# Row sums applied to the exponentials before they are turned; 5 of 16 copies between quadrants issued by ScalarE

## Chip, cores and metric

One core of one Trainium2 chip. The time is that of one launch in device microseconds (us); the kernel before is given as the median of three runs, and its profile is of one further execution. Smaller is better.

## What is computed

All arrays are float32. B, H, S, D = 4, 8, 576, 64; 2304 tokens, d_model 512, d_ff 2048.

```python
scores = scale * q @ k.T                               # per batch and head, 576 x 576
thresh = max(scores, axis=-1) - tau
scores = where(scores >= thresh, scores, -1e9)
attn   = exp(scores - max(scores, axis=-1))
attn   = attn / (sum(attn, axis=-1) + 1e-9)
x      = attn @ v                                      # then heads side by side: 2304 x 512
h = x @ w_in;   x = where(h > 0, h, exp(min(h, 0)) - 1) @ w_out      # first layer
h = x @ w2_in;  out = max(0.01 * h, h) @ w2_out                      # second layer
```

## The kernel before, in words

**Stages.** The first stage, up to about 520 us of the span, is the attention, with part of the first layer laid between its steps (7 blocks of 256 tokens, the first half of d_ff). Then come the rest of the first layer and the second layer, which are almost nothing but matmuls in blocks of 512 tokens.

**Attention.** The work is cut into 32 *groups*: 8 token ranges (4 or 5 *units* of 64 query rows each) times 4 pairs of heads; 144 units in all. `group` (line 417) issues the loads of k, q and v on SyncE's queue (SP), then its units. A unit (line 435) runs, for 64 query rows of both heads on 128 partitions: the scores `s` by TensorE (PE; line 442); scale and row extreme into `ss` by VectorE (DVE; 446); threshold `thr` by DVE or GpSimd (POOL; 449, 451); mask and exponential `e` by ScalarE (ACT; 454, 457), the latter with the row sum `su`; then `e` has to be turned so that keys lie on partitions. In the first 4 groups PE turns it (472). In the other 28, DVE turns 32 x 32 blocks within each quadrant of 32 partitions (464, `e` to `t`), and 16 DMA copies move the blocks between quadrants (486, `t` to `p`). These copies can begin when all units of the group are turned. Then PE multiplies `p` with `v` (496) and DVE multiplies the result with the reciprocal row sums `rb` into `x` (504). Buffers: 2 each of `t`, `p`, `e`, `k`, `q`, `v`, `s`; 3 of `ss`; one PSUM bank for the product with `v`.

**Row sums.** After the product the query rows lie along the free axis, so the reciprocals have to be turned and spread too. `row_sums` (line 509) does it once a group: reciprocal (511) and a 32 x 32 transpose (512) on DVE, a store to DRAM (513), and two loads that broadcast it over 64 partitions each (515), all on SP's queue. Line 504 waits for these loads.

**Order.** The source does not fix the order of instructions. A list scheduler (`Order.run`) places every step by readiness, by a due time (offsets in the table `KN`) and by an assumed cost, and picks an engine where a step has alternatives (`ka`, `kx`, `kg`, ... in `KN` name them: P, A, D for POOL, ACT, DVE). On the chip each engine works through its own list strictly in that order. The assumed cost of a DMA issue on SP is `ISSUE`.

**The two MLP layers.** Steps `h` (548; PSUM `h` and `hb`) and `y` (591) are float32 products made of three passes over a high and a low part (`xh`, `xl`, `gh`, `gl`, `wih`, ...), which ACT, DVE and POOL split (helpers in lines 298 to 310). The second half of the first layer's weights is loaded and split once the attention has ended.

Of the kernel before, what the change touches and what calls it, by code (L numbers as in the profile page):

```python
# [10 lines left out]
F32 = mybir.dt.float32  # L11
# [10 lines left out]
NP = NH // 2  # L22
# [11 lines left out]
BESIDE = 7  # L34
GP = 1
SX = 640
LAG = 2
# [5 lines left out]
KN = dict(  # L43
    pad=18, stay=3577.21, late=1.3, margin=0, look=0.00390102, warm=3, tu=2231.35, lead=16053.3, wv0=828.315,
    wv1=194.793, early=4257.91, boff=24778.1, bdt=4649.72, yoff=2581.02, coff=-6478.49, wb=1663.97, w2a=5835.19,
    o1=-2909.85, o2=1357, o3=2931.81, o4=-3826.63, o5=5331.7, o6=-25.7749, mo=-10678.1, ka='PA', kl='PAD', kh='PA',
    ko='D', kt='DP', kx='A', kxl='DP', km='DP', kg='AD', kgl='P', kgl1='D', kd='P', kc='AD')

# [41 lines left out]
class Order:  # L90
# [5 lines left out]
    def op(self, alts, deps=(), uses=(), vt=0.0, lat=0.0):  # L96
        o = Op()
        o.alts = alts if isinstance(alts, list) else [alts]
        o.deps, o.vt, o.lat = [d for d in deps if d is not None], vt, lat
        o.outs, o.done, o.eng, o.seq = [], None, None, len(self.ops)  # L100
        for g in uses:
            if g.back is not None:
                o.deps.append(g.back)
            if not g.users and g.before is not None:
                o.deps.append(g.before.users[0])
            g.users.append(o)
        self.ops.append(o)
        return o

    def run(self):  # L110
        for o in self.ops:
            deps = set()
            for d in o.deps:
                deps.update(d.users if isinstance(d, Gen) else (d,))
# [111 lines left out]
LAND = 2100.0  # L226
ISSUE = 350
HALFP = 105
# [20 lines left out]
def moved(packets, size):  # L249
    return packets * (6 + size * 0.0385) / 16 * 1.35  # L250

@with_exitstack
def attn_moe_kernel(ctx, tc, qT, kT, vn, tau, w1i, w1o, w2i, w2o, yp, rsd, out):
    nc = tc.nc
# [34 lines left out]

    def sp(packets, size, fn):  # L290
        return (SP, ISSUE, fn, moved(packets, size))

# [69 lines left out]
    k_r = ring(ap_, 2, [128, 2, HALF], F32, "k")  # L362
    q_r = ring(ap_, 2, [128, 2, 64 * UM], F32, "q")
    v_r = ring(ap_, 2, [128, 2, 5, D], F32, "v")
# [7 lines left out]
    e_r = Ring(itertools.cycle(es_).__next__, 2)  # L372
    ident = ac.tile([128, 128], F32, name="ident")
    make_identity(nc, ident)
    sm_r = {t: ring(ap_, 4, [128, 1], F32, t) for t in ("nm", "thr")}
    su_r = ring(ap_, 3, [128, UM], F32, "su")
    rc_r = Ring(None, 2)
    st_r = ring(ap_, 2, [128, 32], F32, "st")
    rb_r = ring(ap_, 2, [128, 64 * UM], F32, "rb")

# [5 lines left out]
    ss_r.make = itertools.cycle(sts).__next__  # L386
    sus = [ac.tile([128, 32], F32, name=f"rc{j}") for j in range(2)]
    for t in sus:
        nc.vector.memset(t, 1.0)
    rc_r.make = itertools.cycle(sus).__next__  # L390
    wz = sts[0]
# [22 lines left out]
    xready = {}  # L414
    slot = itertools.count()

    def group(gi, p, vts):
# [9 lines left out]
        by_pe = gi < GP  # L427
        su, pg, tg = su_r.new(), p_r.new(), None if by_pe else t_r.new()
        done, turned = [], []

# [3 lines left out]
        def unit(j, vt):  # L434
            s, ss, e = s_r.new(), ss_r.new(), e_r.new()
            nm, thr = (sm_r[t].new() for t in ("nm", "thr"))

            def qk():
                for h in range(2):
                    for i in range(2):  # L440
                        r = slice(64 * i, 64 * i + 64)
                        nc.tensor.matmul(s()[64 * h:64 * h + 64, i, 0:HALF], q()[r, h, 64 * j:64 * j + 64],  # L442
                                         k()[r, h], start=True, stop=True)
# [13 lines left out]
            o = op((ACT, act(S) + 190, lambda: nc.scalar.activation(  # L457
                out=e()[:, 0:S + 1], in_=ss()[:, 0:S + 1], func=AF.Exp, bias=taun, accum_out=su()[:, j:j + 1])),
                [o], [ss, e, su], vt + KN["o2"])
            done.append(o)  # L460
            cols = slice(32 * j, 32 * j + 32)

            if not by_pe:
# [3 lines left out]
                return  # L467
            t = ya.new()

# [12 lines left out]
        vt = vts[n - 1] + KN["o3"]  # L482
        rb, rgot = row_sums(gi * NE + p, n, su, done, vt + 500)
        got = turned
        if not by_pe:
            got = [op(sp(32, 20 * w, lambda a=a, d=d: nc.sync.dma_start(  # L486
                out=pg()[32 * d:32 * d + 32, 5 * a * w:5 * a * w + 5 * w],
                in_=tg()[32 * a:32 * a + 32, 5 * d * w:5 * d * w + 5 * w])), turned, [pg, tg], vt + KN["o4"])
                for a in range(4) for d in range(4)]
            vt += KN["o5"]  # L490
# [10 lines left out]
        def split(a):  # L501
            return a.rearrange("p (h u i) -> p h u i", h=2, i=32)

        xready[gi, p] = op((DVE, dve(64 * n), lambda: nc.vector.tensor_tensor(
            out=x[:, p, b * S + 64 * u0:b * S + 64 * u1].rearrange("p (u h i) -> p h u i", h=2, i=32),
            in0=split(ps()[:, 0:64 * n]), in1=split(rb()[:, 0:64 * n]), op=ALU.mult)),
            [o, *rgot], [ps, rb], vt + KN["o6"] + 500)

    def row_sums(at, n, su, done, vt):
        rb, st, rc = rb_r.new(), st_r.new(), rc_r.new()  # L510
        o = op((DVE, 140, lambda: nc.vector.reciprocal(out=rc()[:, 0:n], in_=su()[:, 0:n])), done, [su, rc], vt)
        o = op((DVE, 140, lambda: nc.vector.transpose(out=st(), in_=rc())), [o], [rc, st], vt)
        o = op(sp(128, 128, lambda: nc.sync.dma_start(out=rsd[at].rearrange("a u i -> (a u) i"), in_=st())),
               [o], [st], vt)
        got = [op(sp(128, 128 * n, lambda h=h: nc.sync.dma_start(  # L515
            out=rb()[64 * h:64 * h + 64, 0:64 * n].rearrange("p (a q) -> p a q", a=2),
            in_=rsd[at, 2 * h:2 * h + 2, 0:n].rearrange("a u i -> a (u i)").partition_broadcast(64))),
            [o], [rb], vt) for h in range(2)]
        return rb, got

# [256 lines left out]
```

## Time and profile before

| | |
|---|---|
| median of 3 runs | 1160.18 us (1159.62 to 1168.07) |
| the profiled execution | 1164.52 us, its span in the trace 1162.7 us |
| busy: PE / DVE / ACT / POOL | 1051.9 / 586.6 / 508.0 / 157.5 us |
| busy share of the 16 DMA engines, SP's and ACT's common queue kind | 37.9% of the span |

A busy share over the whole span mixes the attention stage with the MLP stages, so the stages are read apart. "SPq" is the queue of SyncE, on which an entry is one DMA issue; the time a transfer takes afterwards is not in it. Issuing DMAs isn't counted as busy time of any engine. The releaser of a wait is inferred; of several that could have ended it, the latest is named.

### The profile page before, as it was taken

The page shows a single profiled execution, that of the slowest core. Times are in us where ns is not written, and L with a number is a line of the kernel's source. Part 1 is how long each engine was busy: PE and PEld are TensorE (multiplying, and loading weights), DVE is VectorE, ACT ScalarE, POOL GpSimd, SP SyncE. Part 2 cuts the span into 40 slices and gives each one's busy share as a digit, 9 for nine tenths or more (in the row PEclk, how much of TensorE's full clock was granted, in tenths as well). Part 3 has the DMA queues.
Part 4 walks back from the last instruction along what each step waited for, and adds up shares of the span by engine and source line. Part 5 has one row for each costly group of instructions (what it writes and reads, how often), then busy time and mean ns, then how long its engine had stood idle before and what let it go on. Part 6 is the DMA issues. An engine that isn't in the chain of part 4 may idle for free.

```text
span 1162.7 us, 17064 instructions
## 1 busy us (share of the span) xinstructions
PE 1051.9 (90%) x6294; PEld 814.4 (70%) x6294; DVE 586.6 (50%) x1201; ACT 508.0 (44%) x1006; POOL 157.5 (14%) x278
## 2 busy tenths in 40 slices
PE   7778777787788778889999999999999999999998
PEld 3455455555566555558888888988888888888898
DVE  6876555655566556628888943686121121121121
ACT  6976555555455555515655532453221221221221
POOL 3454121222111122100111100010000000000000
PEclk9989898989899889989999999999999999999999
DMA  6676666656666666543544411132000000000000
GB/s 217 195 214 178 171 179 178 176 136 179 158 176 158 162 178 176 152 123 109 161 132 161 146 36 37 56 120 79 1 37 1 1 37 1 1 37 1 1 37 20
DMA packets 72435, 125.39 MB, mean 108 GB/s; under 512 B 16032, under 2 KB 37024, under 8 KB 72352
## 3 DMA queue, kind: packets, MB, share of 16 engines
q1 hardware_dynamic: 72352, 124.30, 37.9%
q8 instruction: 50, 0.82, 0.3%
q14 instruction: 33, 0.27, 0.1%
HBM read 72.35 MB, written 9.96 MB: 71 GB/s over the span
## 4 chain that ended last, share of the span: by engine, by line
PE 65%; SPq 15%; DMA 9%; DVE 5%; issue 3%; ACT 2%; POOL 0%; DVEq 0%; ACTq 0%; POOLq 0%
PE y L591 29%; PE h L548 15%; PE hb L548 13%; SPq L486 13%; PE v L496 6%; DMA rb<-rsd_dram 2%; DMA rsd_dram<-st 2%; DMA wraw<-in_w1i_dram 2%; PE s L442 2%; DVE ss L446 2%; DMA p<-t 2%; DVE t L464 1%; ACT e L457 1%; SPq L515 1%; SPq L426 1%
## 5 line engine op out<-in xcount | busy, mean ns | idle before, releaser
L591 PE MATMUL y<-gh,woh 128*128 128x512 f32 (+1 forms) x736 | 255.6, 347 | 2.1 <-ACT ysx L309 1.4
L591 PE MATMUL y<-gl,woh 128*128 128x512 f32 (+1 forms) x736 | 251.4, 342 | 0.0
L591 PE MATMUL y<-gh,wol 128*128 128x512 f32 (+1 forms) x736 | 251.3, 341 | 0.0
L298 DVE TENSOR_TENSOR gl<-g,gh 128x512 fp32r<-128x512 f32 (+1 forms) x128 | 83.3, 651 | 270.6 <-ACT g L574 260.9
L496 PE MATMUL v<-p,v 128*64 128x320 f32 (+1 forms) x640 | 127.9, 496 | 68.8 <-DMA rsd_dram<-st 39.1
L548 PE MATMUL h<-xh,wih 128*128 128x256 f32 (+1 forms) x480 | 164.6, 343 | 14.1 <-DVE g L567 9.4
L591 PEld LDWEIGHTS y<-gh,woh 128*128 128x128 f32 x736 | 138.5, 188 | 34.7 <-issue 14.4
L548 PE MATMUL h<-xl,wih 128*128 128x256 f32 (+1 forms) x480 | 159.0, 331 | 1.3 <-POOL xl L299 1.0
L548 PE MATMUL h<-xh,wil 128*128 128x256 f32 (+1 forms) x480 | 158.3, 330 | 0.0
L454 ACT ACTIVATE ss<-ss,thr 128x576 f32<-128x576 f32 x144 | 110.3, 768 | 105.5 <-DVE thr L451 58.2
L591 PEld LDWEIGHTS y<-gl,woh 128*128 128x128 f32 x736 | 138.6, 188 | 16.2
L591 PEld LDWEIGHTS y<-gh,wol 128*128 128x128 f32 x736 | 138.6, 188 | 16.2
L496 PEld LDWEIGHTS v<-p,v 128*64 128x64 f32 x640 | 62.7, 162 | 122.5 <-issue 64.1
L446 DVE TENSOR_SCALAR_CACHE_REDUCE ss<-s,scl 128x576 f32<-128x576 f32 x144 | 115.1, 800 | 46.6 <-PE s L442 45.3
L464 DVE STREAM_TRANSPOSE t<-e 128x640 f32<-128x640 f32 x128 | 106.7, 839 | 44.7 <-DMA rsd_dram<-st 19.0
L548 PEld LDWEIGHTS h<-xh,wih 128*128 128x128 f32 x480 | 91.6, 191 | 43.4 <-DVE g L567 12.3
L457 ACT ACTIVATE e<-ss,taun 128x577 f32<-128x577 f32 x144 | 111.5, 774 | 13.4 <-DVE t L464 11.1
L442 PE MATMUL s<-k,q 64*64 64x288 f32 x1152 | 97.6, 442 | 12.9 <-DVE ss L446 8.7
L548 PEld LDWEIGHTS h<-xl,wih 128*128 128x128 f32 x480 | 91.8, 191 | 10.2 <-POOL xl L299 1.5
L548 PEld LDWEIGHTS h<-xh,wil 128*128 128x128 f32 x480 | 91.9, 191 | 8.2
L548 PE MATMUL hb<-xl,wih 128*128 128x512 f32 (+1 forms) x256 | 94.5, 369 | 0.0
L548 PE MATMUL hb<-xh,wil 128*128 128x512 f32 (+1 forms) x256 | 94.5, 369 | 0.0
(438 smaller groups left out, 1139.7 us busy)
## 6 DMA issues: line engine op xcount, KB each, us to landing
p<-t SPq DMA_DIRECT2D x256, 100.0 KB, 2.2
p<-t SPq DMA_DIRECT2D x192, 80.0 KB, 2.4
v<-in_vn_dram SPq DMA_DIRECT2D x32, 320.0 KB, 3.7
k<-in_kT_dram SPq DMA_DIRECT2D x32, 288.0 KB, 3.0
wraw<-in_w1i_dram SPq DMA_DIRECT2D x16, 512.0 KB, 4.4
wraw<-in_w1o_dram SPq DMA_DIRECT2D x16, 512.0 KB, 3.6
wraw<-in_w2i_dram SPq DMA_DIRECT2D x16, 512.0 KB, 3.5
wraw<-in_w2o_dram SPq DMA_DIRECT2D x16, 512.0 KB, 3.4
```

The source lines that it names most:

```text
L298: return pick(who, D=(dve(n), lambda: nc.vector.tensor_tensor(**args()), PORT), P=(pool_tt(n), lambda: nc.gpsimd.tensor_tensor(**args())))
L426: lv = op(sp(128, 2560, lambda: nc.sync.dma_start(out=v(), in_=vn[hp])), [], [v], due + 8e3)
L442: nc.tensor.matmul(s()[64 * h:64 * h + 64, i, 0:HALF], q()[r, h, 64 * j:64 * j + 64], k()[r, h], start=True, stop=True)
L446: o = op((DVE, dve(S) + 160, lambda: nc.vector.tensor_scalar(out=ss()[:, 0:S].rearrange("p (j c) -> p j c", j=2), in0=s()[:, :, 0:HALF], s ...
L454: o = op((ACT, act(S) + 95, lambda: nc.scalar.activation(out=ss()[:, 0:S], in_=ss()[:, 0:S], func=AF.Prelu, bias=thr(), scale=-1.0, alpha= ...
L457: o = op((ACT, act(S) + 190, lambda: nc.scalar.activation(out=e()[:, 0:S + 1], in_=ss()[:, 0:S + 1], func=AF.Exp, bias=taun, accum_out=su( ...
L464: turned.append(op((DVE, dve(SX) + 70, lambda: nc.vector.transpose(out=blocks(tg).rearrange("p d c q -> p c d q")[:, :, :, cols], in_=e(). ...
L486: got = [op(sp(32, 20 * w, lambda a=a, d=d: nc.sync.dma_start(out=pg()[32 * d:32 * d + 32, 5 * a * w:5 * a * w + 5 * w], in_=tg()[32 * a:3 ...
L496: nc.tensor.matmul(ps()[64 * h:64 * h + 64, 0:64 * n], v()[:, h, c, :], blocks(pg)[:, 2 * h:2 * h + 2, c], start=(c == 0), stop=(c == 4))
L515: got = [op(sp(128, 128 * n, lambda h=h: nc.sync.dma_start(out=rb()[64 * h:64 * h + 64, 0:64 * n].rearrange("p (a q) -> p a q", a=2), in_= ...
L548: nc.tensor.matmul(hp(), w_()[:, cs], x_()[:, 0:tb], start=(k == 0 and z == 0), stop=(k == KC - 1 and z == 2))
L591: nc.tensor.matmul(ysl(yg, m), w_()[:, cs], g_()[:, 0:tb], start=(first and z == 0 and share == 0), stop=(last and z == 2 and end))
```

## The change

The reciprocal of each unit's row sum is taken on DVE right after the exponential, and `e` is multiplied with it before it is turned; `row_sums`, its store and its two loads a group go, and the product with `v` is copied to `x` by ACT (`kv='A'`). `kn='P'` gives the new multiplication to POOL. Of a group's 16 copies 5 are issued by ACT (`NA`), spread over the 16. `e` gets a third buffer. q is laid out so that a group's load has 128 pieces in place of 256. The scheduler's table has new due times and other choices of engine, and assumes 640 for a copy's issue on SP (before 350) and 300 on ACT.

```diff
+NA = 5
+ACTI = 300
...
-    o1=-2909.85, o2=1357, o3=2931.81, o4=-3826.63, o5=5331.7, o6=-25.7749, mo=-10678.1, ka='PA', kl='PAD', kh='PA',
-    ko='D', kt='DP', kx='A', kxl='DP', km='DP', kg='AD', kgl='P', kgl1='D', kd='P', kc='AD')
+    o1=-2774.74, o2=2563.78, o3=4792.89, o4=-1365.21, o5=3801.46, o6=-25.7749, mo=-2531.64, ka='PA', kl='PAD',
+    kh='PAD', ko='PD', kt='DP', kx='AD', kxl='DP', km='DP', kg='P', kgl='P', kgl1='D', kd='P', kc='AD', kn='P',
+    kv='A')
...
-    es_ = [ac.tile([128, SX], F32, name=f"e{j}") for j in range(2)]
+    es_ = [ac.tile([128, SX], F32, name=f"e{j}") for j in range(3)]
...
-              op(sp(256, 256 * n, lambda: nc.sync.dma_start(
-                  out=q()[:, :, 0:64 * n], in_=qT[hp][:, :, 64 * u0:64 * u1])), [], [q], due)]
+              op(sp(128, 512 * n, lambda: nc.sync.dma_start(
+                  out=q()[:, 0:128 * n], in_=qT[hp][:, 128 * u0:128 * u1])), [], [q], due)]
...
             o = op((ACT, act(S) + 190, lambda: nc.scalar.activation(
-                out=e()[:, 0:S + 1], in_=ss()[:, 0:S + 1], func=AF.Exp, bias=taun, accum_out=su()[:, j:j + 1])),
+                out=e()[:, 0:S + 1], in_=ss()[:, 0:S + 1], func=AF.Exp, bias=taun, accum_out=su())),
                 [o], [ss, e, su], vt + KN["o2"])
-            done.append(o)
+            o = op((DVE, 150, lambda: nc.vector.reciprocal(out=su(), in_=su())), [o], [su], vt + KN["o2"])
+            o = op(pick(KN["kn"], P=(pool_ts(S) + 90, lambda: nc.gpsimd.tensor_scalar(
+                            out=e()[:, 0:S], in0=e()[:, 0:S], scalar1=su(), scalar2=1.0, op0=ALU.mult, op1=ALU.mult)),
...
-        rb, rgot = row_sums(gi * NE + p, n, su, done, vt + 500)
         got = turned
         if not by_pe:
-            got = [op(sp(32, 20 * w, lambda a=a, d=d: nc.sync.dma_start(
...
+            for z, (a, d) in enumerate((a, d) for d in range(4) for a in range(4)):
...
+                if z * NA // 16 != (z + 1) * NA // 16:
+                    got.append(op((ACT, ACTI, lambda copy=copy: copy(nc.scalar)), turned, [pg, tg], vt + KN["o4"],
+                                  lat=2500))
+                else:
+                    got.append(op(sp(32, 20 * w, lambda copy=copy: copy(nc.sync), 640), turned, [pg, tg],
+                                  vt + KN["o4"]))
...
-        xready[gi, p] = op((DVE, dve(64 * n), lambda: nc.vector.tensor_tensor(
...
-    def row_sums(at, n, su, done, vt):
...
+        xready[gi, p] = op(copy_of(KN["kv"], 64 * n, lambda: x[:, p, b * S + 64 * u0:b * S + 64 * u1].rearrange(
+            "p (u h i) -> p h u i", h=2, i=32), lambda: split(ps()[:, 0:64 * n])), [o], [ps], vt + KN["o6"] + 500)
```

Over the program the lists change so: 144 reciprocals of one column on DVE in place of 32 of 4 or 5 and 32 small transposes; 144 multiplications of `e` on POOL; 32 multiplications into `x` on DVE become 32 copies on ACT; 140 copies between quadrants are issued on ACT and 308 on SP; 96 DMAs of the row sums go. The 56 steps `gh<-g` of the first stage, before 42 on ACT and 14 on DVE, are all on POOL; POOL computes 100 of the 144 thresholds (before 77).

SP's queue in the middle of the attention stage, before: `rsd_dram<-st` and `rb<-rsd_dram` are the store and the loads of the row sums, `p<-t` the copies between quadrants, one group's with `t_88`.

```order
L513 DMA rsd_dram<-st 128x32
L423 DMA k<-in_kT_dram 128x576
L424 DMA q<-in_qT_dram 128x2x256
L486 DMA p<-t_88 32x640 x6
L515 DMA rb<-rsd_dram 64x2x128 x2
L486 DMA p<-t_88 32x640 x5
L426 DMA v<-in_vn_dram 128x640
L486 DMA p<-t_88 32x640 x5
```

And SP's queue in such a place after the change.

```order
L501 DMA p<-t_87 32x640 x6
L429 DMA v<-in_vn_dram 128x640
L501 DMA p<-t_87 32x640 x5
L501 DMA p<-t_88 32x640 x3
L426 DMA k<-in_kT_dram 128x576
L427 DMA q<-in_qT_dram 128x640
L501 DMA p<-t_88 32x640 x3
L429 DMA v<-in_vn_dram 128x640
L501 DMA p<-t_88 32x640 x5
```

A group has 11 copies on SP where it had 16, and no DMA of the row sums stands among them.

DVE in the attention stage, before: the multiplication into `x` (L504), which reads `rb`, stands among the units' steps.

```order
L446 TENSOR_SCALAR ss_102,nm<-s,scl 128x576
L504 TENSOR_TENSOR x<-v,rb 128x2x4x32
L446 TENSOR_SCALAR ss_103,nm<-s,scl 128x576
L567 SCALAR_TENSOR_TENSOR g<-g,h 128x256
L464 STREAM_TRANSPOSE t_87<-e_90 128x5x4x32
L305 TENSOR_SCALAR gh<-g 128x256
L567 SCALAR_TENSOR_TENSOR g<-g,h 128x256
L511 RECIPROCAL rc_105<-su 128x4
```

DVE after the change, in such a place.

```order
L450 TENSOR_SCALAR ss_105,nm<-s,scl 128x576
L473 STREAM_TRANSPOSE t_87<-e_90 128x5x4x32
L464 RECIPROCAL su<-su 128x1 x2
L473 STREAM_TRANSPOSE t_87<-e_91 128x5x4x32
L450 TENSOR_SCALAR ss_106,nm<-s,scl 128x576
L464 RECIPROCAL su<-su 128x1
L450 TENSOR_SCALAR ss_104,nm<-s,scl 128x576
L473 STREAM_TRANSPOSE t_88<-e_89 128x5x4x32
```

No instruction of DVE's units waits behind a DMA's landing for `x` any more; a reciprocal stands between the exponential and each transpose, with POOL's multiplication between the two.

ACT after the change: the 5 copies of a group stand together between the activations of the units, and the copy into `x` among them.

```order
L461 ACTIVATE e_89,su<-ss_104,taun 128x577
L501 DMA p<-t_88 32x640 x5
L458 ACTIVATE ss_105<-ss_105,thr 128x576
L565 ACTIVATE g<-h 128x256
L461 ACTIVATE e_90,su<-ss_105,taun 128x577
L458 ACTIVATE ss_106<-ss_106,thr 128x576
L314 COPY x<-v 128x2x4x32
L461 ACTIVATE e_91,su<-ss_106,taun 128x577
```

Before, ACT issued no DMA at all; what is behind the first of the five waits with it until the group's last transpose is done.

## Rows read from the trace of the kernel before

**Rows 1.** Stretches: busy of PE, PEld, DVE, ACT, POOL; granted clock, DMA share, GB/s.
```profile
75.00:520.00 445.00, 358.63 (x2782) 246.11 (x2782) 249.54 (x587) 230.95 (x487) 94.48 (x190) 0.92 0.64 167
100.00:500.00 400.00, 320.87 (x2504) 219.18 (x2503) 226.63 (x534) 211.53 (x447) 79.98 (x168) 0.92 0.64 166
530.00:1163.00 633.00, 628.62 (x3044) 532.07 (x3042) 273.09 (x456) 212.83 (x388) 27.50 (x34) 1.00 0.17 55
```

**Rows 2.** Chain that ended last, 75 to 505 us, shares by line.
```profile
by line: SPq L486 30.1%; PE v L496 14.1%; issue 6.5%; DMA rsd_dram<-st 5.4%; DMA rb<-rsd_dram 5.2%; PE h L548 5.1%; PE s L442 4.5%; DMA p<-t 4.3%; PE y L591 4.0%; DVE ss L446 3.1%; DVE t L464 2.5%; SPq L515 2.0%; DMA wraw<-in_w1i_dram 1.5%;
```

**Rows 3.** Timeline of SP's queue, 213 to 232 us: start, length, line, what.
```profile
213.07 0.52 SPq L513 DMA_DIRECT2D rsd_dram<-st  x1
213.69 0.39 SPq L423 DMA_DIRECT2D k<-in_kT_dram  x1
214.12 0.63 SPq L424 DMA_DIRECT2D q<-in_qT_dram  x1
214.91 1.29 SPq L515 DMA_DIRECT2D rb<-rsd_dram  x2
...
217.75 0.33 SPq L426 DMA_DIRECT2D v<-in_vn_dram  x1
222.00 10.11 SPq L486 DMA_DIRECT2D p<-t  x16
```

**Rows 4.** Timeline of DVE in the same stretch; idle time before in brackets.
```profile
219.99 0.49 DVE L504 TENSOR_TENSOR x<-v,rb 128x320 f32<-128x320 f32 x1 [4.71 <-DMA rb<-rsd_dram]
...
221.13 0.84 DVE L464 STREAM_TRANSPOSE t<-e 128x640 f32<-128x640 f32 x1
```

**Rows 5.** Line 486 from 75 to 520 us: duration min/median/max in ns.
```profile
L486 SPq DMA_DIRECT2D p<-t x432: 507/590/2044, 80.0 to 512.5; - x144
```

**Rows 6.** Waits from 100 to 500 us, releaser behind the arrow: total, times, longest.
```profile
DVE x L504 <- DMA rb<-rsd_dram: 47.4, 16, 7.5
PE v L496 <- DMA rsd_dram<-st: 35.8, 14, 3.4
PE v L496 <- DMA p<-t: 12.3, 8, 3.7
PE v L496 <- DVE x L504: 7.1, 2, 5.4
PE v L496 <- DMA k<-in_kT_dram: 5.0, 1, 5.0
PE s L442 <- DMA q<-in_qT_dram: 3.6, 4, 1.3
```

**Rows 7.** Timeline of PE: two groups' products with `v`.
```profile
185.10 5.07 PE L496 MATMUL v<-p,v 128*64 128x256 f32 x20 [5.36 <-DVE x L504]
...
200.33 2.91 PE L496 MATMUL v<-p,v 128*64 128x320 f32 x20
```

**Rows 8.** The stretch of the first of these, columns as rows 1.
```profile
184.00:191.00 7.00, 5.90 (x36) 3.72 (x36) 4.16 (x12) 4.35 (x9) 0.99 (x2) 0.58 0.78 225
```

**Rows 9.** Copies between quadrants: count, KB each, median us to landing.
```profile
p<-t SPq DMA_DIRECT2D x256, 100.0 KB, 2.2
```

**Rows 10.** Groups by line and shape, 75 to 520 us: count, busy us, mean ns.
```profile
L511 DVE RECIPROCAL rc<-su 128x4 f32<-128x4 f32 x12 | 1.9, 155 | 0.0
L564 POOL TENSOR_SCALAR g<-g 128x256 f32<-128x256 f32 x43 | 17.4, 404 | 93.6 <-ACT g L560 93.3
L304 ACT ACTIVATE gh<-g 128x256 fp32r<-128x256 f32 x41 | 16.9, 411 | 28.1 <-DVE g L567 27.9
L560 ACT ACTIVATE g<-h 128x256 f32<-128x256 f32 x53 | 20.0, 378 | 33.1 <-PE h L548 31.4 <-DVE g L567 1.2
```

**Rows 11.** POOL's one-input operations of 512 columns: shortest and longest.
```profile
L302 POOL TENSOR_SCALAR woh<-wb__215 x1: 617/617/617, 16.3 to 16.3; 128x512 fp32r<-128x512 f32 x1
L321 POOL TENSOR_SCALAR wa__721<-wraw x1: 1174/1174/1174, 53.7 to 53.7; 128x512 f32<-128x512 f32 x1
```

More of the change, by code (lines that the diff above doesn't have):

```diff
@@ L35 @@
 GP = 1
+AHEAD = 2
+PT = ()
+NA = 5
+ACTI = 300
 SX = 640
@@ L104, in op @@
             if not g.users and g.before is not None:
-                o.deps.append(g.before.users[0])
+                o.deps.append((g.before,))
             g.users.append(o)
@@ L113, in run @@
             for d in o.deps:
-                deps.update(d.users if isinstance(d, Gen) else (d,))
+                deps.update(d.users if isinstance(d, Gen) else d[0].users[:1] if isinstance(d, tuple) else (d,))
             deps.discard(o)
@@ L226 @@
 LAND = 2100.0
-ISSUE = 350
+ISSUE = 400
 HALFP = 105
@@ L252, in attn_moe_kernel @@
 @with_exitstack
-def attn_moe_kernel(ctx, tc, qT, kT, vn, tau, w1i, w1o, w2i, w2o, yp, rsd, out):
+def attn_moe_kernel(ctx, tc, qT, kT, vn, tau, w1i, w1o, w2i, w2o, yp, out):
     nc = tc.nc
@@ L288, in attn_moe_kernel, with sp @@
     PORT = True
-    def sp(packets, size, fn):
-        return (SP, ISSUE, fn, moved(packets, size))
+    def sp(packets, size, fn, issue=ISSUE):
+        return (SP, issue, fn, moved(packets, size))
     def pick(who, **alts):
@@ L362, in attn_moe_kernel @@
     k_r = ring(ap_, 2, [128, 2, HALF], F32, "k")
-    q_r = ring(ap_, 2, [128, 2, 64 * UM], F32, "q")
+    q_r = ring(ap_, 2, [128, 128 * UM], F32, "q")
     v_r = ring(ap_, 2, [128, 2, 5, D], F32, "v")
@@ L386, in attn_moe_kernel @@
     ss_r.make = itertools.cycle(sts).__next__
[L387 to L390, printed above, removed]
     wz = sts[0]
@@ L414, in attn_moe_kernel, with s_of @@
     xready = {}
-    slot = itertools.count()
+    slots, unit_no = [], itertools.count()
+    def s_of(i):
+        while len(slots) <= i and len(slots) < NP * NU:
+            slots.append(s_r.new())
+        return slots[i] if i < len(slots) else None
     def group(gi, p, vts):
@@ L423, in group @@
         ld = [op(sp(128, 2304, lambda: nc.sync.dma_start(out=k(), in_=kT[hp])), [], [k], due),
-              op(sp(256, 256 * n, lambda: nc.sync.dma_start(
-                  out=q()[:, :, 0:64 * n], in_=qT[hp][:, :, 64 * u0:64 * u1])), [], [q], due)]
+              op(sp(128, 512 * n, lambda: nc.sync.dma_start(
+                  out=q()[:, 0:128 * n], in_=qT[hp][:, 128 * u0:128 * u1])), [], [q], due)]
         lv = op(sp(128, 2560, lambda: nc.sync.dma_start(out=v(), in_=vn[hp])), [], [v], due + 8e3)
-        by_pe = gi < GP
-        su, pg, tg = su_r.new(), p_r.new(), None if by_pe else t_r.new()
-        done, turned = [], []
+        by_pe = gi < GP or p in PT
+        pg, tg = p_r.new(), None if by_pe else t_r.new()
+        turned = []
         def blocks(g):
@@ L434, in unit @@
         def unit(j, vt):
-            s, ss, e = s_r.new(), ss_r.new(), e_r.new()
-            nm, thr = (sm_r[t].new() for t in ("nm", "thr"))
+            un = next(unit_no)
+            s, ss, e = s_of(un), ss_r.new(), e_r.new()
+            nm, thr, su = (sm_r[t].new() for t in ("nm", "thr", "su"))
             def qk():
@@ L467, in unit @@
                 return
-            t = ya.new()
+            s_of(un + AHEAD)
+            t = (ya if gi < GP else s_r).new()
             def tr():
@@ L482, in group, with copy @@
         vt = vts[n - 1] + KN["o3"]
-        rb, rgot = row_sums(gi * NE + p, n, su, done, vt + 500)
         got = turned
         if not by_pe:
-            got = [op(sp(32, 20 * w, lambda a=a, d=d: nc.sync.dma_start(
-                out=pg()[32 * d:32 * d + 32, 5 * a * w:5 * a * w + 5 * w],
-                in_=tg()[32 * a:32 * a + 32, 5 * d * w:5 * d * w + 5 * w])), turned, [pg, tg], vt + KN["o4"])
-                for a in range(4) for d in range(4)]
+            got = []
+            for z, (a, d) in enumerate((a, d) for d in range(4) for a in range(4)):
+                to = pg, slice(32 * d, 32 * d + 32), slice(5 * a * w, 5 * a * w + 5 * w)
+                fr = tg, slice(32 * a, 32 * a + 32), slice(5 * d * w, 5 * d * w + 5 * w)
+                def copy(q, to=to, fr=fr):
+                    q.dma_start(out=to[0]()[to[1], to[2]], in_=fr[0]()[fr[1], fr[2]])
+                if z * NA // 16 != (z + 1) * NA // 16:
[4 more added lines that the diff above has]
+                                  vt + KN["o4"]))
             vt += KN["o5"]
```

36 lines of the change are left out of this document (11 added, 25 removed).

## Prediction

> **What bounds the kernel now.** I read the stretches first. From 530 us on PE is busy 628.6 of 633 us at full granted clock [rows 1]: nothing the change touches can be gained there. From 75 to 520 us PE is busy only 358.6 of 445 us, so 86.4 us are idle, and the granted clock is 0.92. The attention stage is therefore the place. No compute engine fills it: DVE 249.5, ACT 231.0, POOL 94.5 of 445.
>
> Next the chain of waits over that stage [rows 2]: its largest share, 30.1%, is SP's queue issuing the 16 copies of line 486; the DMAs of the row sums and their issue take another 12.6%. The timeline of SP's queue shows why [rows 3]. Sixteen copies hold it 10.11 us, 0.632 each, one behind the other (the issue itself 0.59 in the median [rows 5]). With the store 0.52, k 0.39, q 0.63, two loads of `rb` 1.29 and v 0.33 a group costs SP 13.27 us. The stretch from 75 to 520 us holds 432 copies [rows 5], 27 groups, so a group takes 445 / 27 = 16.5 us. SP is thus issuing 80% of the time, and its entries wait for landings and buffers in the rest.
>
> The third view is the waits of PE and DVE [rows 6]. DVE stands 47.4 us before `x`, until the loads of `rb` land, and strict order makes the next unit's steps stand behind it: at 219.99 us it had been idle 4.71 us, two units' steps followed, and only behind the transpose at 221.13 could the next 16 copies start, at 222.00 [rows 3, 4]. The row sums and the copies so close a ring: copies, store, loads, `x`, transpose, copies. PE stands 35.8 + 12.3 us before its product with `v`. The first number carries the store's name, but by the code the product waits for v and the 16 copies alone; the store is issued just behind the last copy and lands with it. I take both as waits for the copies. With 7.1 for `x`, 5.0 for k and 3.6 for q, SP's queue and the row sums own 63.8 of the 79.1 us that PE is idle from 100 to 500 us (400 less 320.87 [rows 1]), 81%, which makes 70 of the 86.4.
>
> **The change, part by part.** *SP's queue.* A group loses 5 copies, 3.16 us, the store and two loads, 1.81: SP needs 13.27 - 4.97 = 8.3 us a group, where PE is busy 358.6 / 27 = 13.3. SP stops being the bound, and PE is what is late next. Of the 70 us of PE's waits I take three quarters away, 52: the ring through `x` is gone and the copies are all issued 3.2 us sooner, but each group's last copy still has to land, 2.2 us [rows 9], when PE may have nothing else. The ends are one third (only the ring and the row sums' entries help) and all of it: 23 and 70.
>
> *Clock.* With two levels, 1.2 and 2.4 GHz, a mean of 0.92 means 16% of 445 us, 71 us, at the low one, which at the high level would take 36 us less. The low level follows PE's waits: the product of 185.10 us, after 5.36 us idle, takes 5.07 us in a stretch with clock 0.58, and a longer one at 200.33 takes 2.91 [rows 7, 8]. If 52 of 86 us of idle time go, I take a third of the 36 back: 12, ends 0 and 30.
>
> *ACT.* It gets 5 issues a group. No row shows a DMA issued by ACT. From below it is 0 or a little less, if ACT's queue issues while an activation runs; the nearest row is the same copy on SP, 0.632 with the gap; I take that. ACT loses 42 `gh` steps of 0.411 [rows 10], 0.63 a group, and gains a copy into `x`, some 0.43 (0.378 at 256 columns [rows 10], scaled half way to 320). So ACT needs 231.0 / 27 - 0.63 + 0.43 + 3.16 = 11.5 us a group, below PE's 13.3: cost 0 as long as it stands little at the copies.
>
> *POOL and DVE.* A multiplication of `e` has 576 columns: 0.404 at 256 and 0.617 at 512 [rows 10, 11] make about 0.70; the ends are 0.617 and 1.174, the shortest and longest at 512 [rows 11]. POOL then has 3.5 + 4.5 x 0.70 + 0.85 (56 `gh` of 0.404 over 27 groups) + 0.23 for more thresholds = 7.7 us a group. DVE loses `x`, the old reciprocal and the small transpose, and gains 4.5 reciprocals of at most 0.155 [rows 10], 0.70 a group; it stays near its 9.2. Neither is a bound. The unit's path grows by 0.155 + 0.70 = 0.86 us, which units behind one another hide as long as `e` has a free buffer, and it has three now. Uncovered at each group's last unit it would cost 27 x 0.86 = 23 us, or 27 x 1.33 = 36 with the long multiplication. I take 0, since the copies of one group are then being issued while the next group's units run.
>
> The Trainium skill (SBUF — State Buffer, "SBUF: two separate sides") speaks against this part: VectorE and GpSimd share a pair of ports as an exclusive lock, and who comes second blocks for the whole instruction. By that rule the multiplication would often cost the 1.174 of the long row; the two durations of one operation in rows 11 agree with it, and the sum would then lose up to the 36 us.
>
> *Start and end.* The first 4 groups, before 75 us, also get the longer path: 0, ends +13 (16 units, 0.86 each) and -5 (their row sums' DMAs go). At the end, the last group's copies are issued 3.2 us sooner and its `x` waits for no load: 4 us less, ends 0 and 8. After 530 us PE has no slack to win or, with DVE at 273 and ACT at 213 of 633 us, to lose: 0, ends -5 and +5 for the changed splits of weights.
>
> **Sum.** 52 + 12 + 4 = 68 us less than the profiled 1164.5 us, 1096.5. That execution stands 4.3 us above the median of the runs, 1160.2, so the median of the changed kernel is forecast at 1092 us.
>
> **Rivals.** *A: the copies come no sooner.* If issues by SP and ACT exclude one another, or the DMA engines, busy 0.64 already and 0.78 in a denser stretch [rows 1, 8], stretch the landings as issues get denser, a group's 16 copies still take 10.1 us. Then only the ring and the row sums' entries go: half of the 70, 35, with 6 of the clock and 2 at the end, 43 us, 1117. For it: nothing shows two queues issuing together. Against it: 143 to 225 GB/s were moved in different stretches, so the engines have some room.
>
> The Trainium skill has a rule that makes this a rival with a mechanism (Perfetto Trace Analysis, "DMA Instruction — HWDGE (DVE, Sync)"): a queue's issue includes waiting for a descriptor generator that the sequencers share and lock. By that rule moving copies to ACT saves SP nothing, and case A's 1117 is the result; no run here shows it.
>
> *B: all of it goes.* PE keeps working through, all 70 us of waits and 24 of the clock go, with 4 at the end: 98 us, 1062. For it: the scheduler's assumed cost of a copy on SP, 350 before, is now 640 beside a measured 632, so the lists fit the chip better. Against it: new steps in the unit's path.
>
> *C: the multiplication of `e` is in the way.* It stands uncovered with its long duration: 36 us on the forecast, 1128. For it: POOL works in strict order, and thresholds of later units queue behind multiplications that wait for DVE. Against it: POOL is under 60% of PE's need.
>
> *D: slower; ACT stands at the copies.* ACT's five copies stand at the head of its queue until the group's last unit is through the reciprocal, multiplication and transpose (0.155 + 0.70 + 0.84 [rows 4] = 1.7 us), until earlier transfers have landed (2.2), and until the product that frees `p` is done (2.9 [rows 7]): 6.8 us a group with all the following units' activations behind them. ACT would need 11.5 + 6.8 = 18.3 us a group, 1.8 more than the 16.5 now: 27 x 1.8 = 49 us, 1209. It decides from 16.5 - 11.5 = 5.0 us of standing a group. Against it: the scheduler puts the copies where it takes them to be ready, and such a sum needs all three waits unhidden every time.
>
> *E: nothing.* That the copies don't move is excluded: 140 of 448 are in ACT's list. A change within 1% would need C or D to eat the gain by chance.
>
> **Chances.** Forecast 0.48, A 0.18, B 0.15, C 0.09, D 0.06, E 0.04. A measurement here tells about 1%, 11.6 us, from no change. A and C lie below 1148.6 and count as faster but for 0.02 which their spread puts within 1%: faster 0.88, within 1% 0.06, slower 0.06. The range takes in A, B and C with the unknown costs, and leaves out D, E and the far ends: 1056 to 1140.
>
> **What would show it.** Right: the attention stage, 520 us long, ends near 450; SP's queue issues about 8 us a group; PE is idle 35 us or so after the start and the clock is near 0.95; the waits of DVE `x` on `rb` are gone, and those of PE before the product with `v` are under 20 us. An issue on ACT of 0.6 us with SP's at 0.59 would speak against A, SP's rising above 0.8 for it. Wrong: long idle time of ACT ended by DVE's transpose or DMA landings (D), PE waiting behind POOL's multiplication (C), or a stage that is no shorter though SP's queue is free.

## The result and the profile after

The changed kernel takes 1114.74 us in the median of four runs (1112.37 to 1115.81), beside 1162.08 us for the kernel before: the ratio is 0.9583 [0.954, 0.9625]. 1092 was forecast with a range of 1056 to 1140; the sign and the range held, but the gain is 47 us where the forecast's sum had 68. The profiled execution took 1115.81 us. Experiments showed that the parts of the change do not add up: without ScalarE's five copies it is worth 80 us (1086.73 beside 1167.11 us of the kernel before, in the runs of that experiment), and the copies give 28 of these back.

The stretches of the changed kernel, with columns as in [rows 1]:

```profile
75.00:472.00 397.00, 339.94 (x2808) 247.76 (x2808) 241.47 (x611) 225.60 (x482) 213.87 (x385) 0.94 0.66 177
...
480.00:1113.00 633.00, 629.86 (x3048) 533.12 (x3048) 286.38 (x504) 196.57 (x358) 21.30 (x21) 1.00 0.17 55
```

Against [rows 1], the last 633 us are as full as before, as forecast. The attention stage ends near 472 us in place of 520. PE is idle 57 us in it (397 less 339.94), where 86.4 stood before and some 35 were expected. The granted clock rose from 0.92 to 0.94 only.

What holds the stage now is read from the chain of waits, 75 to 460 us, shares by line:

```profile
by line: DMA p<-t 19.2%; PE v L515 13.5%; PE h L553 11.8%; PE y L596 7.1%; PE s L446 6.6%; ACTq L501 6.5%; ACT e L461 4.8%; ACT ss L458 4.3%; DMA v<-in_vn_dram 4.2%; SPq L501 4.1%; issue 3.4%; DVE t L473 3.1%; DMA q<-in_qT_dram 1.6%; DVE g 
```

SP's issues of the copies, 30.1% in [rows 2], are down to 4.1%. In their place stand the landings of the copies (19.2%; 4.3% before) and ACT's issues of them (6.5%).

The copies of line 501 by queue, 75 to 472 us (count, issue min/median/max in ns), who waited for them, and their time from issue to landing, which answer to [rows 5, 9]:

```profile
L501 SPq DMA_DIRECT2D p<-t x305: 507/589/1936, 75.4 to 463.5; - x153
L501 ACTq DMA_DIRECT2D p<-t x136: 514/602/2011, 75.8 to 459.8; - x136
...
who waited for it (us, times):
  ACT e L461: 28.2, 9
  ACT g L565: 22.2, 6
  ACT ss L458: 18.9, 6
...
DMA to landing us min/median/max: 2.0/3.0/6.8
```

An issue costs ACT 0.602 us, near the 0.632 taken with SP's gap, and SP's is unchanged at 0.589. What was not foreseen is the middle: ACT's own steps, `e`, `g` and `ss`, have 69 us of idle time before them, 21 times, that ends with a copy's landing. None of them reads a copy's result; they stand behind copies in ACT's list. Issuing is not counted as busy, so most of this idle time is the issues themselves: by their times in the trace, the five issues of a group take 3.3 us in the mean, and the gaps between them 0.8 us.

The waits from 100 to 500 us, which answer to [rows 6]:

```profile
ACT x L314 <- PE v L515: 24.9, 17, 7.9
...
ACT e L461 <- DMA p<-t: 22.6, 7, 5.1
ACT g L565 <- DMA p<-t: 22.2, 6, 4.6
...
ACT ss L458 <- DMA p<-t: 16.8, 5, 4.3
...
PE v L515 <- DMA p<-t: 12.7, 4, 5.8
```

And those of SP's queue from 100 to 472 us:

```profile
SPq L429 <- PE v L515: 45.8, 14, 7.0
SPq L501 <- DMA p<-t: 32.8, 30, 4.5
```

DVE's 47.4 us before `x` are gone. SP's queue now stands too: for the product that frees `v`, and 30 times a copy on SP waits until an earlier copy has landed. By the source a copy needs only the turned units and a free `p`; the copy that it waits for is one of the same kind. The last section has what the trace shows of the reason.

One place shows both queues. SP, and then ACT, in the same stretch (idle time before in brackets):

```profile
232.13 8.72 SPq L501 DMA_DIRECT2D p<-t  x10
...
242.39 8.03 SPq L501 DMA_DIRECT2D p<-t  x6
```

```profile
242.39 5.61 ACTq L501 DMA_DIRECT2D p<-t  x5
248.05 0.78 ACT L461 ACTIVATE e<-ss,taun 128x577 f32<-128x577 f32 x1 [5.14 <-DMA p<-t]
```

ACT's five issues, 3.0 us at 0.602 each, take 5.61, since two of them are long (0.87 and 2.01 us) and the last starts 1.0 us after the end of the one before it; SP's six, 3.5 us, take 8.03, with a gap of 4.5 us before the third. ACT does nothing else for 5.14 us, and the exponentials of the next group's units stand behind.

### The profile page after: what moved, and what is told of

Read it like the earlier page. It is cut to its first block, busy times and chain, and to the rows that moved or that the text cites. A ratio compares the mean times of both kernels' runs of the same rounds, so it can differ in the third digit from the quotient of the medians.

```text
span 1113.7 us, 17058 instructions
## 1 busy us (share of the span) xinstructions
PE 1030.2 (92%) x6294; PEld 812.9 (73%) x6294; DVE 589.8 (53%) x1275; ACT 482.3 (43%) x959; POOL 281.2 (25%) x474
## 4 chain that ended last, share of the span: by engine, by line
PE 71%; DMA 10%; ACT 7%; DVE 5%; ACTq 2%; issue 2%; SPq 2%; POOL 1%; DVEq 0%; POOLq 0%
PE y L596 31%; PE h L553 18%; PE hb L553 14%; DMA p<-t 7%; PE v L515 5%; PE s L446 3%; ACT e L461 2%; ACTq L501 2%; ACT ss L458 2%; DMA v<-in_vn_dram 1%; SPq L501 1%; DVE t L473 1%; DMA wraw<-in_w1i_dram 1%; DVE ss L450 1%; POOL e L465 1%
## 5 line engine op out<-in xcount | busy, mean ns | idle before, releaser
L553 PE MATMUL h<-xh,wih 128*128 128x256 f32 (+1 forms) x480 | 166.9, 348 | 33.9 <-DVE g L572 14.8
L465 POOL TENSOR_SCALAR e<-e,su 128x576 f32<-128x576 f32 x144 | 109.0, 758 | 40.9 <-DVE su L464 40.2
L515 PE MATMUL v<-p,v 128*64 128x320 f32 (+1 forms) x640 | 97.3, 445 | 15.6 <-DMA p<-t 13.8
L553 PE MATMUL hb<-xh,wih 128*128 128x512 f32 (+1 forms) x256 | 94.5, 369 | 0.0
```

Source lines behind the costliest of these rows:

```text
L465: o = op(pick(KN["kn"], P=(pool_ts(S) + 90, lambda: nc.gpsimd.tensor_scalar(out=e()[:, 0:S], in0=e()[:, 0:S], scalar1=su(), scalar2=1.0, o ...
L515: nc.tensor.matmul(ps()[64 * h:64 * h + 64, 0:64 * n], v()[:, h, c, :], blocks(pg)[:, 2 * h:2 * h + 2, c], start=(c == 0), stop=(c == 4))
L553: nc.tensor.matmul(hp(), w_()[:, cs], x_()[:, 0:tb], start=(k == 0 and z == 0), stop=(k == KC - 1 and z == 2))
```

## The experiments

Theory T, formed on these rows: SP's queue was the bound before and the row sums' part frees it, but ACT's copies cost more than they save, by the hole they make in ACT's strict order and by waits of the two queues for each other's landings. Rivals: the copies' landings are the new bound wherever they are issued (a form of A); the buffers of `v` are (45.8 us above); the multiplication is (C); the gain comes from the ring through `x` alone. Ratios are to the kernel before, measured on the same chip.

*How much the order alone moves.* One number of the scheduler's table, a little extra cost for some steps, is shifted:

```diff
-    pad=18,
+    pad=19,
```

> A control: the changed kernel with 19 for 18 in one assumed cost of the scheduler (a constant added to every step of ScalarE, VectorE and GpSimd), so that only the order of instructions moves. If single orders matter little, 1107 to 1122 us (within 0.7% of the changed kernel); how far it lies off is what a new order alone can do, and no difference of another run that is smaller counts.

Measured 1121.87 us, 0.9612 [0.9555, 0.9668]. Another order of the same work moves the median by 7 us, so no smaller difference counts below. This is one other order; a third could move it further.

*All copies on SP.*

```diff
-NA = 5
+NA = 0
```

> The changed kernel with all 16 copies of a group issued by SyncE again, row sums still applied ahead of the turning. Theory 1 (both parts are needed, the queue of SyncE was the bound): SyncE needs 16 x 0.63 + 1.35 = 11.5 us a group instead of 8.3, copies queue up again, and the time goes back by a third to a half of the gain, to 1125 to 1145 us. Theory 2 (the row sums' store and loads were the whole of it, and what ScalarE's copies bring it loses by standing at them): 1105 to 1120 us, the same as the changed kernel within 1%.

Measured 1086.73 us, 0.9326 [0.9286, 0.9367]: 28 us faster than the change. The stage's stretch and SP's waits from 75 to 430 us:

```profile
75.00:445.00 370.00, 335.66 (x2800) 238.90 (x2800) 244.36 (x623) 228.05 (x482) 208.16 (x360) 0.98 0.72 193
```

```profile
SPq L429 <- PE v L515: 11.1, 3, 7.3
SPq L501 <- DMA wraw<-in_w1o_dram: 2.3, 1, 2.3
```

PE is idle 34 us, about what the forecast wanted of the change, and the clock is 0.98. No copy waits for a copy. The landings take 3.0 us in the median here too (2.2 before), with one queue issuing. So the longer landing does not come from the second queue, and it is not what holds the change 28 us behind this run. Why it is longer was not tried.

*Only the copies, in the kernel before.*

```diff
-            got = [op(sp(32, 20 * w, lambda a=a, d=d: nc.sync.dma_start(
...
+                if z * NA // 16 != (z + 1) * NA // 16:
+                    got.append(op((ACT, ACTI, lambda copy=copy: copy(nc.scalar)), turned, [pg, tg], vt + KN["o4"],
+                                  lat=2500))
```

> The kernel before with 5 of a group's 16 copies issued by ScalarE and nothing else; row sums still go through DRAM. Theory 1: SyncE's queue needs 10.1 us a group instead of 13.3, but the ring through the loads of the row sums stays; faster than before by 1 to 2.5%, 1133 to 1150 us. Theory 2: the ring sets the time, so 1150 to 1172 us, no change within 1%.

Measured 1153.77 us, 0.9905 [0.9867, 0.9943]. From 100 to 500 us:

```profile
DVE x L513 <- DMA rb<-rsd_dram: 62.9, 18, 7.8
...
ACT e L459 <- DMA p<-t: 29.0, 9, 4.2
```

With SP's queue relieved by the copies alone, DVE waits longer for the row sums (47.4 in [rows 6]), ACT stands at the copies, and 1% is left.

*A third buffer for `v`.*

```diff
-    v_r = ring(ap_, 2, [128, 2, 5, D], F32, "v")
+    v_r = ring(ap_, 3, [128, 2, 5, D], F32, "v")
```

> The changed kernel with three buffers for v in place of two, so that a load of v that stands between two copies on SyncE's queue no longer waits for the product of two groups earlier. Theory 1 (in the changed kernel SyncE's strict order holds the copies back: 45.8 us of waiting of v loads from 100 to 472 us): that wait nearly goes, copies of a group are issued within 8 us instead of 9.9, and the time falls to 1090 to 1108 us. Theory 2 (PE is the bound at its granted clock, or ScalarE's standing): 1110 to 1120 us, no change within 0.5%.

Measured 1116.06 us, 0.9559 [0.9508, 0.961]: no change. But the edit did only part of what it was for. From 100 to 472 us the loads' wait for a buffer, the largest in SP's queue, fell from 45.8 to 30.4 us, and the copies' wait for copies rose from 32.8 to 44.2. So the run does not show what the whole wait costs, and this rival is not excluded by it.

*The hole without the copies.* All copies on SP, but ACT holds itself at that place with four copies of a tile into scratch:

```diff
-NA = 5
+NA = 0
...
+            op((ACT, 5 * ACTI, lambda: [nc.scalar.copy(out=held, in_=tg()[:, 0:800]) for _ in range(4)]), turned, [tg],
+               vt + KN["o4"])
```

> All 16 copies on SyncE as in the run without ScalarE's copies (1087 us), but at the place where ScalarE issued its 5 copies it now makes 4 copies of 128 x 800 of the turned blocks into a tile nobody reads, some 3.0 to 3.8 us, behind the same transposes; no DMA of ScalarE's, no wait for a landing. Theory 3 (ScalarE's strict order: what its five issues cost is the hole of 3 to 4 us a group in which no unit's exponential runs): most of the 28 us comes back, 1105 to 1125 us. Theory 4 (the copies on ScalarE cost by waiting for the landing of other copies, since the queues share completion semaphores, and by holding back SyncE in turn): 1085 to 1097 us.

Measured 1105.12 us, 0.9485 [0.9441, 0.9529]: 18 us above the run with all copies on SP. The four copies, 75 to 450 us:

```profile
L510 ACT COPY held<-t x106: 841/859/867, 86.3 to 449.2; 128x800 f32<-128x800 f32 x106
```

They hold ACT 4 x 0.859 = 3.4 us a group and issue no DMA; no SP entry waits for a copy's landing in this run. So some 18 of the 28 us are the hole in ACT's order alone. The scheduler took the hold for 1.5 us (5 x 300), so this is the price of a hole that the lists do not know in full. The other 10 go with the copies being DMAs, by little more than the control moved.

Where the hole reaches PE is in PE's own waits. The change, 75 to 472 us:

```profile
PE v L515 <- DMA p<-t: 13.8, 5, 5.8
PE h L553 <- DVE g L572: 13.5, 17, 1.5
PE h L553 <- ACT g L565: 12.4, 11, 2.1
PE s L446 <- DVE ss L450: 10.4, 3, 7.2
```

All copies on SP, 75 to 445 us:

```profile
PE v L515 <- DMA p<-t: 12.4, 12, 3.6
PE h L553 <- DVE g L572: 5.7, 10, 0.6
PE h L553 <- ACT g L565: 5.3, 10, 1.1
...
PE s L446 <- DVE ss L450: 1.2, 2, 0.9
```

ACT held, 75 to 450 us:

```profile
PE h L556 <- ACT g L568: 16.0, 17, 2.5
PE h L556 <- DVE g L575: 12.4, 19, 1.3
PE s L447 <- DVE ss L451: 9.7, 5, 5.4
PE v L518 <- DMA p<-t: 2.9, 2, 1.7
```

The wait for the copies themselves, before the product with `v`, is hardly longer in the change than with all copies on SP. What grows, and with the plain hold just as much, are PE's waits before `h`, for the first layer's `g` on ACT and DVE, and before the scores `s`, for DVE's `ss`.

*A truer assumed cost.* The scheduler is told 640 in place of 300 for a copy's issue on ACT:

```diff
-ACTI = 300
+ACTI = 640
```

> The changed kernel, 5 copies on ScalarE, with 640 in place of 300 for the scheduler's assumed cost of an issue there (602 ns measured), so that the lists leave room for the hole. Theory 3: the hole stays, 1105 to 1122 us. Theory 5 (the hole would be harmless if the lists knew of it; the wrong cost is what loses the 28 us): 1085 to 1100 us.

Measured 1104.11 us, 0.9473 [0.9439, 0.9508]: 11 us back, somewhat over the control's 7. With the truer cost the five copies still cost 17 us over none. SP's copies still wait for landings, 29.7 us, 33 times from 75 to 455 us:

```profile
SPq L429 <- PE v L515: 39.3, 14, 6.5
SPq L501 <- DMA p<-t: 29.7, 33, 2.5
```

*Two copies on ACT.*

```diff
-NA = 5
+NA = 2
```

> 2 of 16 copies on ScalarE instead of 5. Without any the queue of SyncE has become the bound again at 12.7 us a group (16 issues and k, q, v back to back) with PE 92% busy. Theory 3: a hole of 1.2 us a group costs two fifths of 28 us, 11, and SyncE gains 1.3 us a group, of which PE at 92% can take half, some 8 us over the stage: 1083 to 1097 us. Theory 4 (each copy on ScalarE brings waits on shared semaphores, whatever their number): 1097 to 1115 us.

Measured 1103.08 us, 0.9469 [0.9442, 0.9495]. ACT's idle time that ends with a landing is nearly gone (5.0 us of `e`, 2.8 of `g`, from 100 to 430 us), but SP's copies wait as long as with five, 75 to 450 us:

```profile
SPq L501 <- DMA p<-t: 32.0, 22, 5.6
```

Two copies already cost 16 us. With none there is no such wait, and the time has no middle optimum among 0, 2 and 5.

*Is the multiplication in the way?* All copies on SP, and DVE multiplies `e` in place of POOL:

```diff
-    kg='P', kgl='P', kgl1='D', kd='P', kc='AD', kn='P',
+    kg='P', kgl='P', kgl1='D', kd='P', kc='AD', kn='D',
```

> All copies on SyncE, and the multiplication of the exponentials on VectorE instead of GpSimd. VectorE, 69% busy in the stage, gets 144 operations of about 0.37 us more, GpSimd loses 144 of 0.76. If the multiplication on GpSimd stands uncovered in the unit's path (rival C), the shorter one wins: 1070 to 1082 us. If it is covered, SyncE's queue at 12.7 us a group sets the time and nothing is won, 1083 to 1100 us, the more the fuller VectorE's list.

Measured 1100.34 us, 0.9444 [0.9424, 0.9464], 14 us slower than with POOL. Taking the multiplication off POOL wins nothing on balance: C has no support. DVE took it at 0.516 us in the median (0.476 to 1.040, 126 of them), not at the 0.37 expected, and is busy 301.40 us of 380 in the stage, where it was 244.36 of 370.

*The ring alone.* The kernel before, with the row sums' DMAs kept, but DVE no longer waits for them: ACT copies the product into `x`, and POOL multiplies it by `rb` there.

```diff
-        xready[gi, p] = op((DVE, dve(64 * n), lambda: nc.vector.tensor_tensor(
+        o = op((ACT, actp(64 * n), lambda: nc.scalar.copy(out=xs, in_=split(ps()[:, 0:64 * n]))),
+               [o], [ps], vt + KN["o6"] + 500)
+        xready[gi, p] = op((POOL, pool_tt(64 * n), lambda: nc.gpsimd.tensor_tensor(
+            out=xs, in0=xs, in1=split(rb()[:, 0:64 * n]), op=ALU.mult)), [o, *rgot], [rb], vt + KN["o6"] + 500)
```

> The kernel before, its 16 copies and the row sums' store and loads all still on SyncE (13.3 us of its queue a group), but VectorE no longer waits for the loads: ScalarE copies the product with v into x, and GpSimd then multiplies x with the reciprocal row sums. Theory 8 (the ring: VectorE standing 47 us before x, with the next units' steps behind it, was what made the 16.5 us a group): 1100 to 1130 us, period of a group near the queue's 13.3 us. Theory 9 (the length of SyncE's queue with the row sums' five entries was it): 1145 to 1170 us, no change within 1.5%.

Measured 1166.97 us, 1.0024 [1.0, 1.0048]: nothing. The standing has moved (100 to 500 us):

```profile
ACT x L505 <- PE v L496: 86.0, 24, 7.4
POOL x L507 <- DMA rb<-rsd_dram: 75.9, 15, 10.1
```

DVE is out of the ring, and the stage is as long as it was. SP's entries are the same as before, which speaks for the queue; since ACT and POOL now stand instead, the ring is not excluded by this run alone.

*SP's queue made longer.* All copies on SP, and three stores a group on SP's queue of a constant tile that nobody reads:

```diff
-NA = 5
+NA = 0
...
+        for z in range(3):
+            op(sp(128, 128, lambda z=z: nc.sync.dma_start(out=rsd[gi * NE + p, z], in_=ones)), turned, [], vt + 500)
```

> All copies on SP, as in e1_na0, and three stores more a group on SP's queue, each of a constant 16 KB tile that nobody reads and nobody waits for. SP's queue theory (in e1_na0 SP's queue is occupied for .97 of the stage at a period of 12.7 us a group, so its issues are the bound, as they were before at 16.5 us): three issues of about .55 to .63 us lengthen each of 27 groups by 1.7 to 1.9 us, 45 to 51 us in all less what hides: 1125 to 1140 us. Rival (the time of a group is set by the ring of dependencies between products, row sums and turning, or by the engines; SP's queue has room): the stores cost nothing that others wait for, 1085 to 1097 us.

Measured 1121.0 us, 0.9616 [0.9597, 0.9634]: 34 us more than without them.

```profile
L496 SPq DMA_DIRECT2D rsd_dram<-ones x96: 319/432/1217, 20.6 to 473.3; - x96
```

That is below the 1125 expected, since an issue took 0.432 us and not 0.55 to 0.63: 27 x 3 x 0.432 = 35 us. The queue's length shows in the time about one to one (give or take the control's 7 us, since the order shifts with it), and the rival's 1085 to 1097 falls.

*SP's queue made shorter.* First the all-SP kernel with two of the table's numbers, those that set when the first weights are loaded, as before:

```diff
-    wv0=3829.45, wv1=-2029.74,
+    wv0=828.315, wv1=194.793,
```

> All copies on SyncE, with the due times of the first weights (two constants) as in the kernel before. The first product with v ends 5 to 6 us later in the changed kernel and in the run without ScalarE's copies than before. Theory 6 (the first weights' later due times make the late start): the first groups end as early as before and the time falls by 4 to 8 us, to 1079 to 1083 us. Theory 7 (the longer path of a unit, reciprocal and multiplication, makes it): 1085 to 1090 us, no change.

Measured 1082.95 us, 0.9293 [0.9262, 0.9324]; 4 us less, within the control. Then, on top of that, k and q side by side in one load, so that SP has one entry less a group:

```diff
-        k, q, v = k_r.new(), q_r.new(), v_r.new()
+        kq, v = kq_r.new(), v_r.new()
+        ld = [op(sp(128, 2304 + 512 * n, lambda: nc.sync.dma_start(
+            out=kq()[:, 0:S + 128 * n], in_=(kqb if u0 else kqa)[hp])), [], [kq], due)]
```

> All copies on SP with the wv tables of before, as in e9_na0_wv (1082.95 us), and k and q of a group lie side by side and come by one load, so SP issues one instruction less a group, about .45 us. SP's queue theory: 27 groups by .45 us, 12 us less at most: 1068 to 1076 us. Rival (SP's queue is not what sets the period at 12.8 us a group, but the engines or the ring of dependencies): 1080 to 1087 us. The control moved 7 us by order alone, so a result between is unclear.

Measured 1080.77 us, 0.9278 [0.9258, 0.9298]. The entry saved did not show. From 200 to 400 us PE was already full, before that edit and after it:

```profile
200.00:300.00 100.00, 92.58 (x805) 66.62 (x804) 68.19 (x177) 64.00 (x135) 55.77 (x101) 1.00 0.73 193
300.00:400.00 100.00, 92.86 (x808) 65.92 (x806) 69.25 (x178) 64.55 (x137) 55.82 (x100) 1.00 0.73 199
```

```profile
200.00:300.00 100.00, 93.00 (x816) 66.85 (x809) 71.20 (x183) 64.88 (x139) 56.23 (x103) 1.00 0.77 199
300.00:400.00 100.00, 94.34 (x820) 66.94 (x818) 68.90 (x179) 65.67 (x141) 57.81 (x105) 1.00 0.79 199
```

The first pair is the run with all copies on SP, the second that with the joint load. At 12.6 to 12.7 us a group SP and PE are level, and a shorter queue has at most the last 6 to 8% of PE to win. The two fastest kernels, these last, stand 32 and 34 us ahead of the change.

The periods of a group, from the ends of successive products with `v` in the traces (15th to last group), put the runs side by side:

| kernel | period, us | time, us |
|---|---|---|
| before | 16.6 | 1162 |
| before, ring opened | 16.8 | 1167 |
| before, 5 copies on ACT | 15.7 | 1154 |
| the change | 14.2 | 1115 |
| all copies on SP, three stores more | 14.2 | 1121 |
| all copies on SP, ACT holds itself | 13.6 | 1105 |
| all copies on SP | 12.7 | 1087 |
| all copies on SP, one load less | 12.6 | 1081 |

## Why the prediction was right, and where it was off

**Right.** The forecast put PE's waits down to SP's queue and the row sums together, and with the row sums gone these waits fell. Which of the two was the bound before is not separated: the queue relieved alone gave 1%, the ring opened alone nothing. The run with three more stores shows that SP's entries become time about one to one where all copies are on SP; by their times in the trace, its entries, one right behind the other, fill 97% of the time there, but 88% in the kernel before and 61% in the change (15th to last product with `v`). DVE's wait on `rb` went, PE's wait before the product with `v` fell from 48 us to 12.7 (under 20 was forecast), ACT's issue is 0.602 us (0.632 was taken), SP's issues are about 8 us a group (11 copies of 0.589, and some 1.5 for k, q and v), and the stretch after 530 us gained nothing. The clock came out at 0.94 for 0.95.

**The sum, term by term.** Over the whole span PE's idle time fell by 27 us (110.8 to 83.5), where 52 of waits and 4 at the end were taken: this term was taken at twice what came. PE's busy time, with the same 6294 matmuls, fell by 22 us (1051.9 to 1030.2), where 12 were taken for the clock. That the forecast lay no more than 23 us off is in part the luck of these two errors.

**ACT: the step that failed.** It says of ACT's need of 11.5 us a group: "cost 0 as long as it stands little at the copies." ACT did stay under the period: 225.60 / 27 = 8.4 us busy, plus 4.1 us from the first of its issues to the end of the last, by their times in the trace, make 12.5 of a period of 14.2. And it stood little: 0.8 us a group between its issues, and in most groups the first issue starts before the activation ahead of it has ended (0.3 us in the median), far from rival D's threshold of 5.0 us. Still the copies cost 28 us, and a plain hold of 3.4 us a group costs 18. A sum of busy time compared with another engine's need doesn't say what a hole costs: the activations behind it come later, and PE waits longer before `h` and `s`, as its rows above show. Of D, the waits at the copies did not come; that the following activations stand behind them did, as a cost on top of the forecast, and D weighed it only as one that turns the sign.

**SP: the wrong entries were priced.** Of the 4.97 us a group taken off SP's queue, the 1.81 of the row sums are worth what they say: three entries put back cost 34 us. The 3.16 us of the five copies are worth less than nothing. With all copies on SP the queue needs 12.7 us, and that was already at PE's level; relief below that had nothing to win. The forecast had both numbers, 13.3 us for PE and 13.27 - 1.81 = 11.5 us for SP without the row sums, and did not put them side by side.

"The copies are all issued 3.2 us sooner" failed as well. From the first issue of a group's copies to the end of the last it took 11.2 us in the mean in the change, 11.8 before and 11.7 with all on SP. SP's copies wait for landings, and loads of k, q and `v` with waits of their own stand between them. What shrank is the time between groups.

**What the all-SP run is made of.** Of its 80 us, 34 come back with three stores; with the store and loads as long as they were, 27 x 1.81 = 49 would, by an estimate at the same rate. The other 31 were not taken apart: the new table, the assumed 640 for SP's issue, q in half as many pieces and the ring's end are all in them.

**Start.** Taken as 0 (ends +13 and -5). By the ends of the products with `v` the 5th group is through at 100.4 us of the launch where it was at 89.8, the 11th at 185.1 where it was at 184.9. So the start is up to 10.6 us late, inside the bound, and the gain begins only behind the 11th group. One cause was tried, in the run with the first weights' numbers as before: there the first product ends at 36.1 us (38.8 in the change, 33.3 before), but the 5th group is through at 100.1. So the first weights are not what makes the 5th group late; the cause stays open, the longer path of a unit among the candidates.

**Multiplication and C.** POOL's took 0.749 us in the median (0.736 to 1.272, 121 of them), beside 0.70 taken, and it costs nothing that the run with DVE could win back. The prediction set against its 0.70 the Trainium skill's exclusive lock between VectorE and GpSimd (SBUF — State Buffer, "SBUF: two separate sides"); by the page the lock is taken, on VectorE's side, only by operations in a 2-port mode or with two SBUF inputs, a condition that the prediction left out. The median is near the short row of [rows 11], and only the longest reached the other.

**Rival A.** That the two queues' issues exclude one another is not seen: with both issuing, SP's copies took 0.589 us as before. From the start times in the trace, issues that overlap one on the other queue have medians of 0.602 us on ACT and 0.585 on SP, those alone 0.603 and 0.589. The Trainium skill's shared, locked descriptor generator (Perfetto Trace Analysis, "DMA Instruction — HWDGE (DVE, Sync)"), which the page describes for VectorE's and SyncE's sequencers, therefore did not show between SP and ACT at this density. But what A said would follow did come: a group's copies come no sooner, by the waits for landings, and landings are longer, 3.0 us for 2.2. Both hold for the run with all copies on SP as well (11.7 and 3.0 us), which is 28 us faster, so they are not why the change landed near A's 1117; a reader of the time alone would have called A right. **B**'s 1062 was reached by no run; the all-SP ones came nearest, at 1081 to 1087.

## What to carry to other kernels

Before moving an issue from a full queue to a compute engine, compare the queue's length after the rest of the change with the next bound: here 12.7 us a group was enough, and the moved copies could only cost. An issue on an engine that works in strict order is priced by what stands behind it, and not by whether that engine has time left: holding ACT 3.4 us a group cost 18 us, though without the hold ACT was busy 62% of the stage (228 of 370 us). Change one part at a time: together they looked like a smaller success of both.

## What the runs showed that was not expected

Copies of one group on two queues wait for each other's landings: 30 waits, 32.8 us in SP's queue with five on ACT, 22 waits, 32.0 us, with two, and none with all on SP. The kernel before shows none either, and with five copies moved to ACT it has 18, 20.4 us from 100 to 500 us. Nothing in the source asks for them. The semaphores in the traces show the reason. All DMAs, of both queues, report their landing on the same eight semaphores in turn, and a copy is issued only when the DMA that used its semaphore before has landed: 439 of the 448 copies of the change carry that wait on their own semaphore, and 447 of those with all on SP. There the DMA in question was issued at least 4.6 us earlier and has landed (3.0 us). In the change it was issued less than 4.5 us earlier for 107 of SP's 308 copies, down to 2.1 us. Of the gaps before SP's copies, 25 end within 0.2 us behind such a landing of another copy (28.5 us; 17 of these copies are ACT's), and 15 behind one of a load of k, q or `v` (17.4 us). What these waits cost in the kernel's time is not shown apart; the 10 us that the plain hold leaves over are the nearest figure.

A DMA's issue is not a fixed price: the medians on SP are 0.432 us for the stores above and 0.589 for a copy between quadrants.
